# Spectral block on one core: the first run of the last inverse stage stands behind second-stage work of the second sequence, and the second weight is converted sooner

## The chip, the cores and the metric

The kernel runs on one core of one Trainium2 chip. Its five engines take their own instruction lists in order: PE (TensorE, matmuls), DVE (VectorE), ACT (ScalarE), POOL (GpSimd) and SP (SyncE), which in this kernel issues all DMA transfers. They wait for one another by semaphores. The metric is the time of one execution on the device in microseconds; before the change the median of three runs is 1844.56 us (1843.51 to 1845.94).

## The reference

The input x is 8 sequences of 3136 rows by 256 columns, in f32. What is computed, cut to its core:

```python
X = np.fft.rfft(x, axis=1)                       # spectral part
Yr = Xr @ w_r - Xi @ w_i + b_r
Yi = Xr @ w_i + Xi @ w_r + b_i
Yr, Yi = soft_threshold(Yr, 0.01), soft_threshold(Yi, 0.01)
a = np.fft.irfft(Yr + 1j * Yi, n=3136, axis=1)   # f32
mixed = np.real(np.fft.fft(np.fft.fft(a, axis=1), axis=2))
u = a + mixed                                    # mixer
un = (u - mean(u)) / sqrt(var(u) + 1e-6)         # over the 256 columns
out = u + np.maximum(un @ w_ch1, 0) @ w_ch2      # 256 -> 1024 -> 256
```

## The kernel before

A transform of 3136 points is done as two shorter ones, so each sequence b = 0 to 7 goes through three stages. Stage 1 (`p1`) transforms the rows with matmuls against `fwd_f`; ACT copies the result to an xf tile, and SP stores it to DRAM (ad<-xf). Stage 2 goes in four quarters q of eight frequencies each: `rows_f2` loads af and the table tff, `p2_f2` finishes the forward transform (L527, f2 below), `p2_w` multiplies by the complex weights (g_w) and DVE and POOL make the soft threshold (y, m, Y), `p2_yt` transposes Y (g_yt), `p2_g2` makes the first half of the inverse (g_g with table tif; ACT copies it to bev and SP stores it, bd<-bev), and `p2_mix` the mixer (g_mix, mq, stored md<-mq). Stage 3 starts with `p3_norm`: its loads (mt<-md, bf<-bd), the last inverse stage (g_g<-bf,inv_f, L410 in the helper `quarters`), the sum with mt on DVE (ut) and the statistics of the norm. `p3_tr` transposes ut (g_ut) into uth and utl, and two MLP stages multiply by the weights (h, then o). Sequence 0 goes through stage 2 in plain f32 matmuls; from sequence 1 on, an f32 operand is split into a high and a low part (tih and til of tif, say) and three products are summed.

The MLP's weights w1 and w2 come in as eight pieces of 512 KB (raw_w) and are converted on the chip by `split_double` (L200 to L221): one ACT instruction (L200), DVE L201, L203, L205, L207 and L209, and for w2 an ACT cast to the high part w2h (L219) and two DVE instructions to the low part w2l (L220, L221). For w2 `split_double` takes an argument `late`, an instruction of ACT behind which L200 may be issued. Tiles share rooms in SBUF by tag: w2h takes the room with the tag W2 and w2l W3, both held by tiles of stage 1 until these are stored.

What sets the order: each stage is a generator that yields due times, and a heap takes the one with the lowest due time next; `WTIMES` are the due times of the eight weight pieces. A generator can also yield until a key is in the set `done` (`after`). `issue_after` puts an instruction behind another one in the order, and `behind(key, ...)` does so for a DMA issue. A scheduler then fixes each engine's list.

The lines that the change touches most:

```python
quarters(inv_f, groups, w_in[1, 0] if b == 0 and ms[0] == 0 else None)    # L840, p3_norm
behind(3 if b or q else 1, out=tif, in_=c_ti[...])                        # L716, p2_yt
split_double(name, h, l, [(sl, raws.pop(k))], False, ks_in[0, 2 + (k > 5)])   # L942, weights
```

Of the kernel before, what the change touches and what calls it, by code (L numbers as in the profile page):

```python
# [20 lines left out]
D = 256  # L21
# [117 lines left out]
SHAPE, STEP1, STEP = (0.395, 0.569, 0.36), 0.2, 0.25  # L139
START1, LEAD, LAST = 1.61, 1.53, 0.05  # L140
T1, ASK, BEHIND = (1.25, 0.17), 1.16, 3
WTIMES = (1.002, 1.003, 1.151, 1.152, 1.4, 1.44, 1.54, 1.57)
MLAG, NRM, TR = 1.874, -1.239, -0.86


# [1 line left out]
def spectral_block(ctx: ExitStack, tc: tile.TileContext, x, w_ri, b_ri, w1, w2,  # L147
                   c_fwd, c_fwd0, c_inv, c_tf, c_ti, c_cs, c_mask, c_ident, out):
    nc = tc.nc
# [167 lines left out]
    def n2_rows(t, m, n):  # L317

        return t[m:m + n].rearrange("n r c u d -> (r c u) n d")
# [183 lines left out]
    def p2_f2(b):  # L503


        for q in range(4):
            base, STEP, F2W, W0, WW, M0 = clock2(b, q)
            u0 = 8 * q
            yield base
            yield from after(("a", b, q) if b == 0 else ("a", b))  # L510
            if b == 0:
                X = sb.tile([128, 2, 2, 8, S], F32, tag=("Xh", "Xl")[q % 2], bufs=1, name="X")
                Xs = sb.tile([128, 2, 8, S], F32, tag=("Xsh", "Xsl")[q % 2], bufs=1, name="Xs")
                xt[b, q] = X, Xs
            else:
                xt[b, q] = Xh, Xl, Xsh, Xsl = x_tiles()
            afs, tfs = zip(*[rows_f2(b, q, s) for s in range(2)])
            for ui in range(4):
                yield base + STEP * ui * F2W / 4
                us = slice(ui * 2, ui * 2 + 2)  # L520
                lo_x = lo_v if b == 1 and q == 0 else lo_g
                g = gtile("g_f2")
                gf = g[:, :400].rearrange("p (k c s j) -> p k c s j", k=2, c=2, s=2)
                for s in range(2):
                    yield base + STEP * F2W * (ui / 4 + s / 8)
                    for k in range(2):
                        mm = te.matmul(gf[:, k, :, s], afs[s][:, ui * D + k * 128:ui * D + k * 128 + 128],  # L527
                                  tfs[s][:, ui].rearrange("p (c j) -> p c j", c=2), start=True, stop=True)
                    if b == 0 and q == 0 and ui == 0:
                        f2_in[s] = mm.ins  # L530
                        done.add(("f2", s))
                gv = g[:, :400].rearrange("p (k c t) -> p k c t", k=2, c=2)

                def view(t):
                    return t[..., us, :].rearrange("p k c s j -> p k c (s j)" if len(t.shape) == 5 else "p k s j -> p k (s j)")

                if b == 0:
                    xv_ = view(X)
                    sc.copy(xv_, gv)
                    va.tensor_add(view(Xs), xv_[:, :, 0], xv_[:, :, 1])  # L540
                    continue
                xs = sb.tile([128, 2, 2 * S], F32, tag="xs", bufs=2, name="xs")
                xh, xl, xsh, xsl = (view(t) for t in (Xh, Xl, Xsh, Xsl))
                if ui < 3:
                    xx = sb.tile([128, 2, 2, 2 * S], F32, tag="xx", bufs=2, name="xx")
                    sc.copy(xx, gv)
                    sc.copy(xh, xx)  # L547
                    lo_x(xl, xx, xh)
                    va.tensor_add(xs, xx[:, :, 0], xx[:, :, 1])
                else:  # L550
                    im = sb.tile([128, 2, 2 * S], F32, tag="im", bufs=1, name="im")
                    sc.copy(xh, gv)
                    sc.copy(im, gv[:, :, 1])
                    va.tensor_add(xs, gv[:, :, 0], im)
                    lo_v(xl, gv, xh)
                sc.copy(xsh, xs)
                lo_x(xsl, xs, xsh)
# [146 lines left out]
    def p2_yt(b):  # L704

        for q in range(4):
# [4 lines left out]
            for i in range(4):  # L711
                yield base + STEP * (M0 + 0.022 + 0.185 * i)
                s = i // 2
                if i % 2 == 0:
                    tif = sb.tile([100, 4, 98], F32, tag="tif", bufs=2, name="tif")
                    behind(3 if b or q else 1, out=tif, in_=c_ti[:, u0 + 4 * s:u0 + 4 * s + 4, :])  # L716
                    if b == 0:
                        tabs[b, q, s] = tif, None
                    else:
                        tih = sb.tile([100, 4, 98], F32R, tag="tih", bufs=1, name="tih")  # L720
                        til = sb.tile([100, 4, 98], F32R, tag="til", bufs=1, name="til")
                        with tc.issue_after(ks_in[b, q]):
                            sc.copy(tih, tif)
                        lo_v(til, tif, tih)
                        tabs[b, q, s] = tih, til
# [48 lines left out]
    def p3_norm(b):  # L774
# [31 lines left out]
        def load(m, n):  # L806
            mt = sb.tile([128, 4, D], F32, tag="mt", bufs=2, name="mt")
            bfs = [sb.tile([128, 512], F32, tag="bf", bufs=4, name="bf") for _ in range(1 + (n > 1))]
            for r in range(2):
                if n == 1:  # L810
                    nc.sync.dma_start(out=bfs[0][64 * r:64 * r + 64, :D], in_=b_dram[b - 1 + r][m, 0].rearrange("c u d -> (c u) d"))
                else:
                    nc.sync.dma_start(out=bfs[r].rearrange("p (n d) -> p n d", d=D), in_=n2_rows(b_dram[b], m + 2 * r, 2))
            for r in (1, 0):
                bb, n2 = (b - 1 + r, m) if n == 1 else (b, NM * r + m)
                mpn, mmn = (d[0:NH].rearrange("(a n2) d -> a n2 d", n2=N2) for d in m_dram[bb])
# [6 lines left out]
        for ms in pairs + [[NM - 1]] * (b % 2):  # L823
            n = 1 if ms[0] == NM - 1 else 4
            t0, T3 = clock3(b, ms[0])
            yield t0 + T3 * (NRM - 0.5 * (n == 1))
            yield from after(("b", b), ("m", b))
            loads = [load(m, n) for m in ms]
            if n == 1:
                mt, bfs = loads[0]  # L830
                g = gtile("g_g1")
                te.matmul(g[:, :D], inv_f, bfs[0][:, :D], start=True, stop=True)
                add(ms[0], 1, g, mt[:, :1])
                finish(ms[0], 1)
                continue
            if b == 0 and ms[0] == 0:
                yield from after(("w", 1, 0))
            groups = [([gtile("g_g1") for _ in range(2)], [[bfs[r][64 * p:64 * p + 64] for r in range(2)] for p in range(2)], bfs[0][0:1, 0:2])
                      for mt, bfs in loads]
            quarters(inv_f, groups, w_in[1, 0] if b == 0 and ms[0] == 0 else None)  # L840
            parts = [(m + 2 * p, g, mt[:, 2 * p:2 * p + 2]) for m, (mt, bfs), (banks, movs, late) in zip(ms, loads, groups) for p, g in enumerate(banks)]
            for m, g, mt in parts:
                add(m, 2, g, mt)
            for m, g, mt in parts:
                finish(m, 2)

    def p3_tr(b):
        for gi, (g0, z) in enumerate(GROUPS[b % 2]):
            t0, T3 = clock3(b, g0)
            w = z * 128  # L850
            for k in range(2):
                yield t0 + T3 * (TR + k / 4)
                if k == 0:
                    uth = sb.tile([128, 2, 512], F32R, tag="uth", bufs=UTHB, name="uth")
                    utl = sb.tile([128, 2, 512], F32R, tag="utl", bufs=2, name="utl")
# [61 lines left out]
    def weights():  # L917
# [14 lines left out]
        for k, (i, name, sl, src) in enumerate(todo):  # L932
# [6 lines left out]
                l = sb.tile(shape, F32R, tag=f"W{2 * i + 1}", bufs=1, name=name + "l")  # L939
                mlp_w[name] = h, l  # L940
            if i:
                split_double(name, h, l, [(sl, raws.pop(k))], False, ks_in[0, 2 + (k > 5)])  # L942
            elif k % 2:
                mark = (0, k // 2)
                yield from after(("w",) + mark)
# [69 lines left out]
```

## Time and profile before

| what | value |
|---|---|
| median of three runs | 1844.56 us (1843.51 to 1845.94) |
| profiled execution, its own time | 1843.13 us |
| span of the profiled execution | 1841.2 us |
| busy: PE, DVE, ACT, POOL | 1798.6, 1200.5, 807.7, 561.8 us |
| chain of work that ended last | PE 86%, DVE 5%, DMA 4% |
| mean granted clock of PE | 0.993 |

The busy times are shares of the span: PE is busy for 98% of it. The chain is followed back from the last instruction, so its shares say which engine's work set the end. The granted clock is 1.00 at full speed.

### The profile page before, as it was taken

The page shows a single profiled execution, that of the slowest core. Times are in us where ns is not written, and L with a number is a line of the kernel's source. Part 1 is how long each engine was busy: PE and PEld are TensorE (multiplying, and loading weights), DVE is VectorE, ACT ScalarE, POOL GpSimd, SP SyncE. Part 2 cuts the span into 40 slices and gives each one's busy share as a digit, 9 for nine tenths or more (in the row PEclk, how much of TensorE's full clock was granted, in tenths as well). Part 3 has the DMA queues.
Part 4 walks back from the last instruction along what each step waited for, and adds up shares of the span by engine and source line. Part 5 has one row for each costly group of instructions (what it writes and reads, how often), then busy time and mean ns, then how long its engine had stood idle before and what let it go on. Part 6 is the DMA issues. An engine that isn't in the chain of part 4 may idle for free.

```text
span 1841.2 us, 29453 instructions
## 1 busy us (share of the span) xinstructions
PE 1798.6 (98%) x10087; PEld 1498.7 (81%) x10087; DVE 1200.5 (65%) x2619; ACT 807.7 (44%) x1911; POOL 561.8 (31%) x1021
## 2 busy tenths in 40 slices
PE   8987999999999999999999999999999999999998
PEld 5566778888888988888888888888888898878888
DVE  3685686676577766765776667757657767655543
ACT  2664545444445534444444444444444454432222
POOL 0002434333234333343432343423324344222110
PEclk9998999999999999999999999999999999999999
DMA  8856564444436543374515744346533533152211
GB/s 247 272 173 165 165 178 135 148 137 138 130 82 198 159 123 104 97 212 125 172 47 135 215 132 125 104 129 164 159 99 86 169 94 112 56 150 69 59 35 33
DMA packets 157934, 245.61 MB, mean 133 GB/s; under 512 B 24208, under 2 KB 105176, under 8 KB 157528
## 3 DMA queue, kind: packets, MB, share of 16 engines
q1 hardware_dynamic: 157784, 243.72, 45.3%
q8 instruction: 80, 1.31, 0.3%
q14 instruction: 70, 0.57, 0.1%
HBM read 140.79 MB, written 102.86 MB: 132 GB/s over the span
## 4 chain that ended last, share of the span: by engine, by line
PE 86%; DVE 5%; DMA 4%; ACT 1%; SPq 1%; issue 1%; POOL 1%; DVEq 0%; ACTq 0%; POOLq 0%
PE o L175 28%; PE h L175 27%; PE g_w L175 9%; PE g_f L527 5%; PE g_g L175 4%; PE g_yt L730 3%; PE g_g L410 2%; PE g_ut L861 2%; PE g_f L410 2%; PE g_mix L667 1%; DMA out_dram<-total 1%; PE g_f L372 1%; DMA aq<-ev 1%; PE g_mix L669 1%; PE g_w L576 1%
## 5 line engine op out<-in xcount | busy, mean ns | idle before, releaser
L880 DVE SCALAR_TENSOR_TENSOR hl<-h,hh 128x512 fp32r<-128x512 f32 (+2 forms) x416 | 272.1, 655 | 391.2 <-ACT hh L879 386.8
L879 ACT ACTIVATE hh<-h 128x512 fp32r<-128x512 f32 (+2 forms) x416 | 237.7, 572 | 505.7 <-PE h L175 459.4
L175 PE MATMUL o<-hl,w2h 128*128 128x512 f32 (+2 forms) x832 | 328.9, 395 | 2.0 <-DVE hl L880 1.5
L175 PE MATMUL h<-utl,w1h 128*128 128x512 f32 (+2 forms) x832 | 319.0, 383 | 1.3 <-DVE utl L165 1.3
L175 PE MATMUL o<-hh,w2l 128*128 128x512 f32 (+2 forms) x832 | 317.9, 382 | 0.0
L175 PE MATMUL o<-hh,w2h 128*128 128x512 f32 (+2 forms) x832 | 317.3, 381 | 0.0
L175 PE MATMUL h<-uth,w1l 128*128 128x512 f32 (+2 forms) x832 | 316.0, 380 | 0.0
L175 PE MATMUL h<-uth,w1h 128*128 128x512 f32 (+2 forms) x832 | 315.3, 379 | 0.0
L887 POOL TENSOR_TENSOR total<-uth,utl 128x256 f32<-128x256 f32 x200 | 149.6, 772 | 460.6 <-DMA out_dram<-total 244.9
L175 PEld LDWEIGHTS o<-hl,w2h 128*128 128x128 f32 x832 | 156.7, 188 | 49.3 <-DVE hl L880 18.7
L175 PEld LDWEIGHTS h<-utl,w1h 128*128 128x128 f32 x832 | 156.8, 188 | 30.5 <-DVE utl L165 1.7
L175 PEld LDWEIGHTS h<-uth,w1l 128*128 128x128 f32 x832 | 156.7, 188 | 29.5 <-issue 1.6
L175 PEld LDWEIGHTS h<-uth,w1h 128*128 128x128 f32 x832 | 156.9, 189 | 27.7 <-issue 2.4
L175 PEld LDWEIGHTS o<-hh,w2l 128*128 128x128 f32 x832 | 156.5, 188 | 27.2
L175 PEld LDWEIGHTS o<-hh,w2h 128*128 128x128 f32 x832 | 156.9, 189 | 19.8 <-issue 0.8
L527 PE MATMUL g_f<-tff,af 98*128 98x100 f32 x1024 | 139.9, 276 | 2.1 <-DMA af<-aq 1.3
L527 PEld LDWEIGHTS g_f<-tff,af 98*128 98x128 f32 x1024 | 134.2, 195 | 7.8 <-issue 1.7
L593 POOL TENSOR_TENSOR Y<-y,m 128x400 f32<-128x400 f32 x56 | 66.9, 1194 | 208.4 <-DVE m L592 198.6
L590 DVE SCALAR_TENSOR_TENSOR y<-g_w,small,ks 128x400 f32<-128x400 f32 x128 | 80.4, 629 | 54.3 <-PE g_w L175 38.0
L168 POOL TENSOR_TENSOR Xl<-xx,Xh 128x400 fp32r<-128x400 f32 x81 | 88.4, 1092 | 60.3 <-ACT Xh L547 56.8
L761 ACT COPY bev<-g_g 98x512 f32<-98x512 f32 x128 | 74.7, 585 | 40.2 <-PE g_g L175 29.3
L730 PE MATMUL g_yt<-ident,Y 128*100 128x128 f32 x512 | 81.8, 277 | 4.8 <-DVE Y L593 4.6
(162 smaller groups left out, 3269.7 us busy)
## 6 DMA issues: line engine op xcount, KB each, us to landing
bd<-bev SPq DMA_DIRECT2D x128, 196.0 KB
mt<-md SPq DMA_DIRECT2D x192, 128.0 KB
bf<-bd SPq DMA_DIRECT2D x96, 256.0 KB
out_dram<-total SPq DMA_DIRECT2D x88, 256.0 KB
af<-ad SPq DMA_DIRECT2D x56, 392.0 KB
ad<-xf SPq DMA_DIRECT2D x84, 256.0 KB
md<-mq SPq DMA_DIRECT2D x112, 192.0 KB
xf<-in_x SPq DMA_DIRECT2D x39, 512.0 KB
```

The lines of the kernel that those rows point to most:

```text
L168: gp.tensor_sub(out_, full, hi.bitcast(F32))
L175: last = te.matmul(o, l, r, start=start and i == 0, stop=stop and i == 2)
L410: return te.matmul(banks[i][64 * j:64 * j + 64], mat[rows, rows], movs[i][j], start=True, stop=True)
L527: mm = te.matmul(gf[:, k, :, s], afs[s][:, ui * D + k * 128:ui * D + k * 128 + 128], tfs[s][:, ui].rearrange("p (c j) -> p c j", c=2), sta ...
L590: va.scalar_tensor_tensor(y1, gw, bias[:, c, o:o + 1], ks, op0=ALU.add, op1=ALU.add)
L593: (va if b == 0 or o == 0 else gp).tensor_sub(y[:, o, :, c, :], y1, m)
L730: te.transpose(gt[:100, (v * 2 + o) * 128:(v * 2 + o + 1) * 128], y[:, o, place].rearrange("p c j -> p (c j)"), ident)
L761: sc.copy(bev, g[:98])
L861: te.transpose(gv[:, i], ut[:, j, k * 128:(k + 1) * 128], ident)
L879: sc.activation(hh[:, :w], h[:, :w], AF.Relu)
L880: va.scalar_tensor_tensor(hl[:, :w], h[:, :w], 0.0, hh[:, :w].bitcast(F32), op0=ALU.max, op1=ALU.subtract)
L887: gp.tensor_add(total[:, k, cols], uth[:, k, cols].bitcast(F32), utl[:, k, cols].bitcast(F32))
```

## The change

Five edits. The due times of the last four weight pieces, all of w2, are lowered, and the ACT instruction behind which their L200 may be issued becomes that of quarter 1 (and 2) instead of 2 (and 3) of sequence 0. The first inverse run of sequence 0 (four matmuls of L410) may be issued only behind the last f2 matmul of quarter 1 of sequence 1 (`f2_in["last"]`, key "f2"), where before it was behind the first g_w of quarter 0. The tif loads of sequence 1's quarter 0 go behind the first mt load, and wait for a key "norm" that `p3_norm` sets when its first loads are issued. `p3_tr` of sequence 0 waits for a key ("n", 0). The key "bf" of the load in `p3_norm` is set and used nowhere.

```diff
--- before.py
+++ after.py
@@ -139,7 +139,7 @@
 SHAPE, STEP1, STEP = (0.395, 0.569, 0.36), 0.2, 0.25
 START1, LEAD, LAST = 1.61, 1.53, 0.05
 T1, ASK, BEHIND = (1.25, 0.17), 1.16, 3
-WTIMES = (1.002, 1.003, 1.151, 1.152, 1.4, 1.44, 1.54, 1.57)
+WTIMES = (1.002, 1.003, 1.151, 1.152, 1.36, 1.42, 1.48, 1.54)
 MLAG, NRM, TR = 1.874, -1.239, -0.86
 
 
@@ -529,6 +529,9 @@
                     if b == 0 and q == 0 and ui == 0:
                         f2_in[s] = mm.ins
                         done.add(("f2", s))
+                    if b == 1 and q == 1 and ui == 3 and s == 1:
+                        f2_in["last"] = mm.ins
+                        done.add("f2")
                 gv = g[:, :400].rearrange("p (k c t) -> p k c t", k=2, c=2)
 
                 def view(t):
@@ -712,8 +715,10 @@
                 yield base + STEP * (M0 + 0.022 + 0.185 * i)
                 s = i // 2
                 if i % 2 == 0:
+                    if b == 1 and q == 0:
+                        yield from after("norm")
                     tif = sb.tile([100, 4, 98], F32, tag="tif", bufs=2, name="tif")
-                    behind(3 if b or q else 1, out=tif, in_=c_ti[:, u0 + 4 * s:u0 + 4 * s + 4, :])
+                    behind("mt" if b == 1 and q == 0 else 3 if b or q else 1, out=tif, in_=c_ti[:, u0 + 4 * s:u0 + 4 * s + 4, :])
                     if b == 0:
                         tabs[b, q, s] = tif, None
                     else:
@@ -810,7 +815,7 @@
                 if n == 1:
                     nc.sync.dma_start(out=bfs[0][64 * r:64 * r + 64, :D], in_=b_dram[b - 1 + r][m, 0].rearrange("c u d -> (c u) d"))
                 else:
-                    nc.sync.dma_start(out=bfs[r].rearrange("p (n d) -> p n d", d=D), in_=n2_rows(b_dram[b], m + 2 * r, 2))
+                    af_ld["bf"] = nc.sync.dma_start(out=bfs[r].rearrange("p (n d) -> p n d", d=D), in_=n2_rows(b_dram[b], m + 2 * r, 2)).ins
             for r in (1, 0):
                 bb, n2 = (b - 1 + r, m) if n == 1 else (b, NM * r + m)
                 mpn, mmn = (d[0:NH].rearrange("(a n2) d -> a n2 d", n2=N2) for d in m_dram[bb])
@@ -826,6 +831,7 @@
             yield t0 + T3 * (NRM - 0.5 * (n == 1))
             yield from after(("b", b), ("m", b))
             loads = [load(m, n) for m in ms]
+            done.add("norm")
             if n == 1:
                 mt, bfs = loads[0]
                 g = gtile("g_g1")
@@ -834,15 +840,16 @@
                 finish(ms[0], 1)
                 continue
             if b == 0 and ms[0] == 0:
-                yield from after(("w", 1, 0))
+                yield from after("f2")
             groups = [([gtile("g_g1") for _ in range(2)], [[bfs[r][64 * p:64 * p + 64] for r in range(2)] for p in range(2)], bfs[0][0:1, 0:2])
                       for mt, bfs in loads]
-            quarters(inv_f, groups, w_in[1, 0] if b == 0 and ms[0] == 0 else None)
+            quarters(inv_f, groups, f2_in["last"] if b == 0 and ms[0] == 0 else None)
             parts = [(m + 2 * p, g, mt[:, 2 * p:2 * p + 2]) for m, (mt, bfs), (banks, movs, late) in zip(ms, loads, groups) for p, g in enumerate(banks)]
             for m, g, mt in parts:
                 add(m, 2, g, mt)
             for m, g, mt in parts:
                 finish(m, 2)
+            done.add(("n", b))
 
     def p3_tr(b):
         for gi, (g0, z) in enumerate(GROUPS[b % 2]):
@@ -850,6 +857,8 @@
             w = z * 128
             for k in range(2):
                 yield t0 + T3 * (TR + k / 4)
+                if b == gi == 0:
+                    yield from after(("n", 0))
                 if k == 0:
                     uth = sb.tile([128, 2, 512], F32R, tag="uth", bufs=UTHB, name="uth")
                     utl = sb.tile([128, 2, 512], F32R, tag="utl", bufs=2, name="utl")
@@ -939,7 +948,7 @@
                 l = sb.tile(shape, F32R, tag=f"W{2 * i + 1}", bufs=1, name=name + "l")
                 mlp_w[name] = h, l
             if i:
-                split_double(name, h, l, [(sl, raws.pop(k))], False, ks_in[0, 2 + (k > 5)])
+                split_double(name, h, l, [(sl, raws.pop(k))], False, ks_in[0, 1 + (k > 5)])
             elif k % 2:
                 mark = (0, k // 2)
                 yield from after(("w",) + mark)
```

ACT at 63 us, where bev is the copy of sequence 0's inverse half, mq the mixer's copy, xf the copies of stage 1, and raw_w_772 the fifth weight piece (k = 4). Before:

```order
L411 COPY g_f_590<-xf 1x2
L761 COPY bev<-g_g_570 98x512
L671 COPY mq<-g_mix 100x256
L469 COPY xf<-g_f_589 128x512
L469 COPY xf<-g_f_590 128x512
L219 CAST w1h<-cv_w_ut 128x512
L411 COPY g_f_646<-xf 1x2
L219 CAST w1h<-cv_w_ut 128x512
```

and now:

```order
L411 COPY g_f_590<-xf 1x2
L766 COPY bev<-g_g_570 98x512
L200 ACTIVATE cv_w_mt<-raw_w_772 128x512
L674 COPY mq<-g_mix 100x256
L200 ACTIVATE cv_w_mt<-raw_w_869 128x512
L469 COPY xf<-g_f_589 128x512
L469 COPY xf<-g_f_590 128x512
L411 COPY g_f_646<-xf 1x2
L219 CAST w1h<-cv_w_ut 128x512
```

Two L200 of w2 have come in, one ahead of the mq copy and one ahead of the xf copies; before, they stood some 26 us further down, at 89 us.

SP at 135 us, the loads around stage 3's start (md_117 and bd_118 are the DRAM tiles of sequence 0). Before:

```order
L763 DMA bd_118<-bev 98x512 x2
L309 DMA tif<-c_ti 100x392
L818 DMA mt<-md_117 32x4x256
L819 DMA mt<-md_117 32x1024
L818 DMA mt<-md_117 32x4x256
L763 DMA bd_118<-bev 98x512 x2
L819 DMA mt<-md_117 32x1024
L495 DMA af<-ad_116 98x1024 x2
L813 DMA bf<-bd_118 128x2x256 x2
```

and now:

```order
L768 DMA bd_118<-bev 98x512 x2
L495 DMA af<-ad_116 98x1024
L823 DMA mt<-md_117 32x4x256
L824 DMA mt<-md_117 32x1024
L823 DMA mt<-md_117 32x4x256
L768 DMA bd_118<-bev 98x512 x2
L824 DMA mt<-md_117 32x1024
L309 DMA tif<-c_ti 100x392
L495 DMA af<-ad_116 98x1024
L497 DMA tff<-c_tf 98x400
L818 DMA bf<-bd_118 128x2x256 x2
```

The tif load has moved from ahead of the first mt loads to behind the fourth of them, and one af load ahead of them.

PE at 145 us, behind the g_w block of sequence 1's quarter 0. Before:

```order
L175 MATMUL g_w<-Xl,wdh 128x400
L175 MATMUL g_w<-Xh,wdl 128x400
L410 MATMUL g_g_1377<-bf,inv_f 64x512
L410 MATMUL g_g_1378<-bf,inv_f 64x512
L410 MATMUL g_g_1377<-bf,inv_f 64x512
L410 MATMUL g_g_1378<-bf,inv_f 64x512
L730 MATMUL g_yt<-ident,Y 100x128
L527 MATMUL g_f_1461<-tff,af 128x2x50 x4
L527 MATMUL g_f_1474<-tff,af 128x2x50 x4
L730 MATMUL g_yt<-ident,Y 100x128
L527 MATMUL g_f_1496<-tff,af 128x2x50 x4
```

and now:

```order
L175 MATMUL g_w<-Xl,wdh 128x400
L175 MATMUL g_w<-Xh,wdl 128x400
L735 MATMUL g_yt<-ident,Y 100x128
L527 MATMUL g_f_1419<-tff,af 128x2x50 x4
L527 MATMUL g_f_1432<-tff,af 128x2x50 x4
L735 MATMUL g_yt<-ident,Y 100x128
L527 MATMUL g_f_1454<-tff,af 128x2x50 x4
L735 MATMUL g_yt<-ident,Y 100x128 x6
```

and 11 rows further down:

```order
L735 MATMUL g_yt<-ident,Y 100x128 x4
L670 MATMUL g_mix<-cs,eh 100x256
L672 MATMUL g_mix<-cs,el 100x128
L410 MATMUL g_g_1513<-bf,inv_f 64x512
L410 MATMUL g_g_1514<-bf,inv_f 64x512
L410 MATMUL g_g_1513<-bf,inv_f 64x512
L410 MATMUL g_g_1514<-bf,inv_f 64x512
L870 MATMUL g_ut<-ident,ut 128x128 x4
```

The four inverse matmuls of the list (the trace counts each as two) stood right behind g_w; now a g_yt, three f2 groups, six g_yt, a g_g and two g_mix stand ahead of them.

## Rows read from the trace of the kernel before

**Rows 1.** Table by stretch: length, busy us (instructions) PE PEld DVE ACT POOL, PEclk, DMA, GB/s.
```profile
60.00:100.00 40.00, 37.70 (x208) 23.25 (x207) 29.01 (x66) 24.64 (x61) 0.00 (x0) 1.00 0.78 244
...
114.00:130.00 16.00, 10.56 (x50) 8.03 (x49) 14.93 (x40) 8.65 (x23) 0.00 (x0) 0.79 0.32 91
...
145.00:176.00 31.00, 21.55 (x110) 17.82 (x109) 18.74 (x44) 14.65 (x34) 13.74 (x25) 0.72 0.71 177
...
300.00:1841.20 1541.20, 1530.32 (x8663) 1296.59 (x8661) 1002.48 (x2172) 662.23 (x1567) 501.79 (x912) 1.00 0.42 122
```

**Rows 2.** SP timeline, 58 to 78 us: start, us, engine, line, transfer.
```profile
60.67 1.16 SPq L309 DMA_DIRECT2D raw_w<-in_w  x2
```

**Rows 3.** Chain of waits, 25 to 100 us: start, us, what.
```profile
33.53 6.74 DMA raw_w<-in_w
...
84.18 5.24 DMA tff<-c_tf
...
92.94 2.96 DMA ad<-xf
```

**Rows 4.** ACT timeline, 62 to 82 us; in brackets: idle before, and releaser.
```profile
63.24 0.59 ACT L761 COPY bev<-g_g 98x512 f32<-98x512 f32 x1 [0.99 <-PE g_g L757]
63.73 0.38 ACT L671 COPY mq<-g_mix 100x256 f32<-100x256 f32 x1
67.19 1.07 ACT L469 COPY xf<-g_f 128x512 f32<-128x512 f32 x2 [3.09 <-DMA raw_w<-in_w]
```

**Rows 5.** PE timeline, 63 to 100 us.
```profile
67.36 1.51 PE L576 MATMUL g_w<-X,wdf 128*128 128x400 f32 x4
...
70.11 1.09 PE L410 MATMUL g_f<-xf,fwd_f 64*64 64x512 f32 x8
...
75.00 2.82 PE L527 MATMUL g_f<-tff,af 98*128 98x100 f32 x24
...
86.14 1.51 PE L576 MATMUL g_w<-X,wdf 128*128 128x400 f32 x4
```

**Rows 6.** DVE groups, 40 to 130 us: busy us, mean ns, idle before.
```profile
L205 DVE SCALAR_TENSOR_TENSOR cv_w_ut<-raw_w,cv_w_mt 128x512 int32<-128x512 int32 x8 | 5.5, 686 | 0.0
...
L207 DVE TENSOR_SCALAR cv_w_mt<-cv_w_ut 128x512 int32<-128x512 int32 x8 | 3.4, 420 | 0.0
```

**Rows 7.** PE timeline, 117 to 132 us.
```profile
121.70 0.87 PE L664 MATMUL g_mix<-csf,ef 128*100 128x129 f32 x6 [2.51 <-DVE mq L676]
124.64 0.88 PE L730 MATMUL g_yt<-ident,Y 128*100 128x128 f32 x3 [2.06 <-DVE Y L593]
126.38 2.54 PE L664 MATMUL g_mix<-csf,ef 128*100 128x129 f32 x10 [0.86 <-ACT yf L734]
...
129.57 2.12 PE L527 MATMUL g_f<-tff,af 98*128 98x100 f32 x16
```

**Rows 8.** Table by two us (and four), columns of group 1.
```profile
124.00:126.00 2.00, 0.88 (x3) 0.45 (x3) 2.00 (x6) 1.87 (x4) 0.00 (x0) 0.50 0.00 0
```

**Rows 9.** PE timeline, 143 to 176 us.
```profile
153.09 2.10 PE L410 MATMUL g_g<-bf,inv_f 64*64 64x512 f32 x8 [7.39 <-DMA bf<-bd]
155.12 0.45 PE L730 MATMUL g_yt<-ident,Y 128*100 128x128 f32 x1
...
174.28 0.34 PE L175 MATMUL g_w<-Xsh,wrh 128*128 128x400 f32 x1
```

**Rows 10.** Chain of waits, 125 to 176 us.
```profile
142.70 3.40 DMA bd<-bev
...
146.60 6.36 DMA bf<-bd
```

**Rows 11.** SP timeline, 134 to 148 us.
```profile
136.68 2.26 SPq L309 DMA_DIRECT2D tif<-c_ti  x1
...
143.14 0.40 SPq L819 DMA_DIRECT2D mt<-md  x1
```

**Rows 12.** DVE timeline, 142 to 158 us.
```profile
144.53 0.56 DVE L165 TENSOR_TENSOR til<-tif,tih 100x392 fp32r<-100x392 f32 x1
```

## Prediction

> **What bounds the kernel now.** I read the page's busy shares first, then the table by stretch, and after it the timelines of each stretch in which PE stands. The reader is to see two things in the table [rows 1]. From 300 us to the end PE is busy for 1530.32 of 1541.20 us, at full clock: there it is the bound, with 10.9 us of idle in all. The change's instructions lie ahead of 200 us, and behind that both programs issue the same work in the same order on every engine. So what the change wins or loses ahead of 200 us reaches the end nearly whole, and the sum is the shift of PE at the point where the two orders are the same again. The second thing: the stretches that the change touches are those where PE is not the bound. It idles 2.3 us of 60–100 us, 5.4 us of 114–130, and 9.5 us of 145–176, with the granted clock at 0.79 and 0.72 in the last two [rows 1]. Each engine takes its list in order, so I walk along three of them.
>
> **Part A, 63 to 98 us: two conversions come sooner, +11 us.** The first two pieces of the second weight are converted behind the bev copy that ACT starts at 63.24 us [rows 4], about 26 us sooner. On ACT the conversion's first instruction (L200) now stands between that bev copy and the mq copy of 63.73, which waited for nothing but PE. L200 needs raw_w, and SP issued both of those loads at 60.67 [rows 2]. A load of the same size (512 KB) took 6.74 us from issue to landing [rows 3]; by that the first one lands at 60.67 + 6.74 = 67.4 us, and ACT's idle of 3.09 us in before, put down to raw_w and ended at 67.19, says the same [rows 4]. So ACT stands from 63.83 to 67.4 with everything behind L200 queued: the mq copy, the xf copies, the casts of the first weight.
>
> - Step 1. L200 ends near 68.1 (an estimate of 0.7 us for it, from bev's 0.59 on the same number of columns [rows 4]), the mq copy near 68.5, then DVE's small mq instruction, and PE's g_w<-X,wdf (67.36 [rows 5]) starts near 69.5: +2.
> - Step 2. The second L200 stands ahead of the xf copies and waits for DVE to read the buffer of the first; DVE can only begin when L200 ended, and has two instructions of 0.42, a y and one of 0.69 ahead [rows 6]. That puts the xf copies of 67.19 at about 71.5 (+4.4), and with the weight casts and DVE pieces between them the f2 block that starts PE's 70.11 row at about 75.5: +5.4 [rows 5].
> - Step 3. The cast into w2h takes room W2, which the tile of first-stage rows holds until its four stores have landed. The last of them is issued near 77.7 in the shifted schedule, and a store of that kind took 2.96 us [rows 3], so the cast starts at 80.6, ahead of copies that PE's f2 (75.00 [rows 5]) needs: f2 at about 81.7, +6.7.
> - Step 4. The subtraction into w2l does the same on DVE with room W3: stores issued near 91, landed 2.96 to 5.24 us later [rows 3], 94 to 96.2. The y for PE's g_w of 86.14 stands behind it. Two w2l pieces and that y (0.69 + 0.69 + 0.63 less overlap) put g_w at 97 to 98: +11 to +12.
>
> I take +11 for part A. Its bounds: if none of the waits binds, the pieces cost nothing on PE, as DVE has 11 us free in 60–100 us [rows 1]; if the second landing is like the tff load's 5.24, +12.5. The later conversions (k=6, 7) stand where k=4, 5 stood, so the small PE stalls after 90 us stay.
>
> The Trainium skill ("DMA: Bandwidth & Descriptors", section "Anatomy of one DMA") puts a transfer at about 2 us plus its bytes at 436 GB/s; it gives that fit for the GpSimd path. By it 512 KB would land 3.2 us after the issue, at 63.9, and step 1 would cost nothing; the trace's 6.74 us for the same load, with the DMA engines at a share of 0.78 in this stretch [rows 1, 3], speaks against it. It is a rival below, since a landing at 64 can be had from no row.
>
> **Part B, 114 to 130 us: the same two conversions are gone, -3.7 us.** One conversion is three instructions of 0.42 and four of 0.69 us on DVE, 4.0 us [rows 6], and two of them ran from 114.9 to 128 us, where DVE was busy for 14.93 of 16 us [rows 1]. PE waits there three times: 2.51 us for mq, 2.06 for Y (both DVE's), 0.86 for ACT's yf, 5.43 us together, and the clock falls to 0.50 [rows 7, 8]. Without the 8 us, DVE's chain from y to Y is done about 3 us sooner, yet PE's g_mix still has to wait for the mq copies that follow it on ACT. Walking the list, f2 (129.57 [rows 7]) comes at 125.2 to 126.5: a gain of 3 to 4.4, and I take 3.7. The lower bound is 0 (ACT ends last in each of the waits), the upper 5.4 (all idle gone).
>
> **Part C, 145 to 176 us: the first inverse run behind f2, -1.6 us.** PE stands 7.39 us after its g_w block, from 145.7 to 153.09, for the bf load; then come the eight inverse matmuls, and only then a g_yt (155.12) and the f2 of the second sequence [rows 9]. The chain is a bd store of 3.40 us and a bf load of 6.36 [rows 10], whatever PE does. The change lets g_yt, f2, g_g and g_mix of sequence 1 stand ahead of the inverse, so the 7.39 us could be filled, if their inputs are there. They are later than before: the tif load of (1, 0) was issued at 136.68 and now stands behind the last of the first mt loads (143.14 + 0.40) [rows 11]. Landing 3.40 (as bd) to 6.36 us (as bf) later [rows 10], it is there at 147 to 150; I take 147.5, since tif is smaller than either (153 KB). Its cast and DVE's til (0.56, at 144.53 [rows 12]) stand ahead of Y on DVE; til can start at about 148.3, so Y is about 4 us late, and the first g_yt is at about 151 instead of 155.12, the inverse at about 161.4 instead of 153.09. With 4 us of useful work moved ahead and the slow clock (0.72 in the mean [rows 1]) lifted no sooner than before, the two orders are level at about 172.7 instead of 174.28 [rows 9]: -1.6. Bounds: -4 (Y is not delayed by tif, PE's gap shrinks to 3 us) and +4 (the inverse is 8 us late, its output feeds the transposes and the MLP, and these find nothing to fill PE with).
>
> **The sum.** 11 - 3.7 - 1.6 = +5.7 us. The profiled execution took 1843.13 us (span 1841.2 us); with the change 1848.8. The median of the runs, 1844.56, lies 1.4 us above it, so for a median 1850.2; I say 1850. Differences under 0.2% (3.7 us) can't be told from no change here.
>
> **Rivals.**
>
> - *The room waits don't bind (no change).* Step 1 and 2 happen (+5), steps 3 and 4 are covered, since in before the tiles of W2 and W3 had to be written in the same stretch too. For it: DVE and ACT are idle for 11 and 15 us of 60–100 [rows 1]. Against: both instructions are in order ahead of copies that PE needs. 5 - 3.7 - 1.6 = -0.3, 1844.
> - *The conversions fall into idle time (faster).* One mechanism: raw_w lands before ACT comes to L200 at 63.83. Then L200 runs in the 3.09 us in which ACT stands in before [rows 4], the stores keep their times, and the room waits end before their instructions are reached; part A costs about 1 us. For it: a landing in 3.40 us, like the bd store's [rows 10], would be 64.1. Against: the 6.74 and the 3.09. It decides from a landing of about 64.5 on: 1 - 3.7 - 1.6 = -4.3, 1840; with part B at its upper end 1838. The Trainium skill's fit above (3.2 us) would give this case.
> - *The inverse run comes too late (much slower).* Part C at +4 with A as forecast: 11 - 3.7 + 4 = +11, 1856. For it: 8 us of delay for the first MLP inputs. Against: f2 and g_yt of sequence 1 are work that PE has to do anyway.
> - *The wait is only replaced.* In place of the bf load PE waits for Y behind til, 7.39 again, and C is 0: 11 - 3.7 = +7.3, 1852, inside the forecast's own range.
>
> **Chances.** Forecast (with the replaced wait) 0.50, own range 1846.5 to 1854; no change 0.20; faster 0.23; much slower 0.07. Faster by over 0.2%: the faster case, with a little of the no-change case, 0.24. Within 0.2%: no change and the low end of the forecast, 0.22. Slower: 0.54. The range that holds 8 in 10 leaves out the ends of the faster and the much slower case: 1839 to 1855.
>
> **What would show it.** Step 1: on ACT an idle of 3 to 4 us ahead of the first L200 of w2, with releaser raw_w. Steps 3 and 4: the first w2h cast and w2l subtraction with an idle released by the ad stores, and g_w<-X,wdf that was at 86.14 at 97. Part B: DVE busy less than 10 of the 16 us around f2, PE idles there under 2 us. Part C: the gap after the g_w block 5 to 6 us and ended by DVE's Y, not by bf; the first inverse matmul 8 us later in relation to the g_w block. The forecast is wrong if the rows of 70 to 98 us are within 3 us of before: then A failed; or if PE runs on from g_w into g_yt with no gap: then C was too small.

## The result, and the profile after

The changed kernel takes 1859.45 us (median of 4 runs, 1856.96 to 1860.21), the kernel before 1845.25 us beside it: a ratio of 1.0073 (95% interval 1.0056 to 1.0091), some 14 us slower. Run again beside other kernels it took 1860.48 us, 1.0084 (1.0067 to 1.0101). The direction was forecast, the size was not: +5.7 us, with 1846.5 to 1854 as the forecast's own range and 1855 as the upper end of the wider one.

The table by stretch of the changed kernel, as in [rows 1] (columns: length, busy us of PE, PEld, DVE, ACT, POOL, then PEclk, DMA share, GB/s):

```profile
60.00:100.00 40.00, 32.78 (x159) 19.28 (x157) 24.31 (x57) 20.28 (x49) 0.00 (x0) 0.87 0.72 216
...
300.00:1858.40 1558.40, 1547.97 (x8766) 1310.91 (x8764) 1017.15 (x2209) 672.04 (x1593) 509.54 (x928) 1.00 0.42 122
```

In the last row the two kernels are alike: 10.4 us of PE idle from 300 us on, 10.9 before [rows 1]. All of the loss is ahead of it, and most of it in 60 to 100 us, where PE was busy for 37.70 us at full clock and is now for 32.78 at 0.87. Step 1 of the forecast is there, larger than forecast. The load of raw_w on SP, and ACT behind it (compare [rows 2, 4]):

```profile
65.45 1.69 SPq L309 DMA_DIRECT2D raw_w<-in_w  x2
```

```profile
65.42 0.58 ACT L766 COPY bev<-g_g 98x512 f32<-98x512 f32 x1 [0.99 <-PE g_g L762]
72.77 0.66 ACT L200 ACTIVATE cv_w_mt<-raw_w 128x512 f32<-128x512 f32 x1 [6.76 <-DMA raw_w<-in_w]
73.33 0.36 ACT L674 COPY mq<-g_mix 100x256 f32<-100x256 f32 x1
75.53 0.68 ACT L200 ACTIVATE cv_w_mt<-raw_w 128x512 f32<-128x512 f32 x1 [1.84 <-DVE cv_w_ut L205]
...
85.90 0.62 ACT L219 CAST w2h<-cv_w_ut 128x512 fp32r<-128x512 f32 x1 [1.46 <-DMA ad<-xf]
```

ACT ends bev at 66.0 and stands 6.76 us for raw_w; the second L200 waits for DVE's L205 as forecast, and w2h's cast for the ad stores (step 3). On DVE the subtraction into w2l stood too (step 4; this trace names tif as the last to come, the second profile of the kernel the ad stores, with an idle of 4.06 us):

```profile
101.57 1.29 DVE L221 TENSOR_TENSOR w2l<-cv_w_ut 128x512 fp32r<-128x512 f32 x2 [3.84 <-DMA tif<-c_ti]
```

What PE does with that (compare [rows 5, 7, 9]):

```profile
74.01 3.04 PE L579 MATMUL g_w<-X,wdf 128*128 128x400 f32 x4 [4.30 <-DVE mq L679]
76.84 1.91 PE L762 MATMUL g_g<-yf,tif 100*98 100x256 f32 x4
...
87.06 2.92 PE L527 MATMUL g_f<-tff,af 98*128 98x100 f32 x24 [1.32 <-ACT xf L469]
...
103.47 2.62 PE L579 MATMUL g_w<-X,wdf 128*128 128x400 f32 x4 [3.99 <-DVE mq L679]
...
147.04 2.53 PE L527 MATMUL g_f<-tff,af 98*128 98x100 f32 x16
...
167.78 0.45 PE L735 MATMUL g_yt<-ident,Y 128*100 128x128 f32 x1 [4.39 <-POOL Y L603]
...
181.95 1.99 PE L410 MATMUL g_g<-bf,inv_f 64*64 64x512 f32 x8 [0.78 <-ACT low L676]
```

Two gaps of 4.30 and 3.99 us, both ended by DVE's mq, stand where forecast, ahead of the two g_w<-X,wdf. What was not forecast stands right behind them: four matmuls of g_w take 3.04 us in place of 1.51 [rows 5], the next four g_g 1.91 in place of 1.03. That is the half clock, 1.2 GHz: the granted clock of 74 to 88 us is 0.66 in the mean.

A table of landmarks on PE shows where the time goes: starts in us, from the PE timelines. The first column is the kernel before, "again" the second run of the changed one.

| PE row | before | changed | again | conversions alone | inverse alone |
|---|---|---|---|---|---|
| g_w<-X,wdf, the one before the first wait | 58.6 | 60.8 | 57.8 | 58.4 | 60.1 |
| next g_w<-X,wdf (67.36 in [rows 5]) | 67.4 | 74.0 | 71.7 | 68.3 | 68.9 |
| f2 x24 (75.00) | 75.0 | 87.1 | 84.6 | 81.5 | 76.5 |
| g_w<-X,wdf (86.14) | 86.1 | 103.5 | 101.2 | 97.8 | 87.6 |
| f2 x24 | 98.7 | 117.8 | 115.4 | 113.0 | 100.2 |
| last g_w<-X,wdf of sequence 0 | 116.3 | 137.1 | 134.7 | 130.6 | 117.8 |
| f2 x16 (129.57 in [rows 7]) | 129.6 | 147.0 | 144.9 | 140.8 | 131.1 |
| first g_w of sequence 1 | 138.9 | 156.6 | 154.2 | 152.9 | 140.4 |
| 48th o | 211.2 | 229.2 | 228.9 | 221.6 | 214.7 |
| span | 1841.2 | 1858.4 | 1858.2 | 1852.6 | 1844.1 |

The first line is startup: it lies between 57.8 and 60.8 us in these profiles, and shifts below are counted from it (an "again" of 71.7, say, is 71.7 + 0.8 against 67.4).

### The profile page after: what moved, and what is told of

Same layout as the page of the kernel before. It is cut to its first block, busy times and chain, and to the rows that moved or that the text cites. A ratio compares the mean times of both kernels' runs of the same rounds, so it can differ in the third digit from the quotient of the medians.

```text
span 1858.4 us, 29450 instructions
## 1 busy us (share of the span) xinstructions
PE 1811.3 (97%) x10087; PEld 1507.9 (81%) x10087; DVE 1198.8 (65%) x2619; ACT 807.4 (43%) x1911; POOL 560.4 (30%) x1021
## 4 chain that ended last, share of the span: by engine, by line
PE 88%; DVE 5%; DMA 3%; ACT 2%; SPq 1%; issue 1%; POOL 1%; DVEq 0%; ACTq 0%; POOLq 0%
PE o L175 28%; PE h L175 27%; PE g_w L175 9%; PE g_f L527 5%; PE g_g L175 4%; PE g_yt L735 3%; PE g_g L410 2%; PE g_ut L870 2%; PE g_f L410 2%; PE g_w L579 2%; PE g_mix L670 1%; PE g_mix L672 1%; DMA out_dram<-total 1%; DVE ut L784 1%; DMA mt<-md 0%
## 5 line engine op out<-in xcount | busy, mean ns | idle before, releaser
L175 PEld LDWEIGHTS h<-uth,w1h 128*128 128x128 f32 x832 | 156.6, 188 | 27.8 <-issue 2.4
L527 PEld LDWEIGHTS g_f<-tff,af 98*128 98x128 f32 x1024 | 138.3, 201 | 9.0 <-issue 2.1
```

The lines of the kernel that those rows point to most:

```text
L175: last = te.matmul(o, l, r, start=start and i == 0, stop=stop and i == 2)
```

## The experiments

**The two halves of the change.** They can be built apart; PE's order up to 190 us is then that of before or after, but for three g_yt near 72 us that go with the conversions. Conversions alone:

```diff
+WTIMES = (1.002, 1.003, 1.151, 1.152, 1.36, 1.42, 1.48, 1.54)
+split_double(name, h, l, [(sl, raws.pop(k))], False, ks_in[0, 1 + (k > 5)])
 quarters(inv_f, groups, w_in[1, 0] if b == 0 and ms[0] == 0 else None)   # as before
```

> Only the weight conversions are moved (due times and the ACT instruction behind which L200 may go); the first inverse run stays where it was in the kernel before. Theory 1 (nearly all of the loss is the conversions): +13 to +16 us against before, 1858 to 1861, with the PE gaps of about 4 us ahead of both g_w<-X,wdf (at 74 and 103 us) and the half clock behind them as in the changed kernel. Rival (the later inverse run loses its part, +4): +9 to +11 us, 1854 to 1856.

Measured: 1854.15 us, 1.0057 (1.0034 to 1.0079), +10.5 us by the ratio and +8.8 by the medians. That lies at the rival's figure. It does not show that the inverse stage's edit has a part in the loss, as the interval overlaps the changed kernel's. On SP and PE:

```profile
46.79 1.19 SPq L309 DMA_DIRECT2D xf<-in_x  x2
...
59.34 0.92 SPq L309 DMA_DIRECT2D raw_w<-in_w  x2
```

```profile
68.27 1.61 PE L576 MATMUL g_w<-X,wdf 128*128 128x400 f32 x4 [1.01 <-DVE mq L676]
...
76.14 2.03 PE L527 MATMUL g_f<-tff,af 98*128 98x100 f32 x8 [0.56 <-DVE mq L676]
78.10 1.99 PE L410 MATMUL g_f<-xf,fwd_f 64*64 64x512 f32 x8
...
81.54 3.28 PE L527 MATMUL g_f<-tff,af 98*128 98x100 f32 x24
...
97.78 3.04 PE L576 MATMUL g_w<-X,wdf 128*128 128x400 f32 x4 [4.13 <-DVE mq L676]
...
163.79 1.66 PE L410 MATMUL g_g<-bf,inv_f 64*64 64x512 f32 x8 [4.09 <-DMA bf<-bd]
```

Here raw_w was issued at 59.34 and landed at 66.95, and the shifts are those of the forecast: f2 x24 +6.8 (forecast +6.7), g_w at 97.78 +11.9 (forecast 11 to 12). At f2 this is in part luck. The stage-1 group of 70.11 [rows 5] is 4.4 us late where step 2 has 5.4 (and calls it f2), and f2 x24 waits for nothing, where step 3 has it wait for a room. What made up the difference is the half clock, for which the forecast has no term: the stage-1 group of 78.10 takes 1.99 us in place of 1.09, the f2 x8 ahead of it 2.03 in place of 1.03. Then the half clock (3.04) makes it +14.6 at the next f2 x24. At 163.79 the wait for bf is 4.09 us in place of 7.39 [rows 9]: the transfers set that start, so 3.3 us of the lateness are absorbed there.

The inverse stage's edit alone (the weights as in before):

> Only the first inverse run, the tif loads and the first transposes are moved; the weights are converted where they were before. Theory 1: -2 to +1 us against before, since PE still waits 4 to 5 us behind the g_w block, now for Y. Prediction on record: -1.6 us (-4 to +4). Rival (the inverse comes too late and the MLP starts late): +4 us. 60 to 145 us should be as in the kernel before, startup included, if the slower startup seen in the changed kernel's trace has nothing to do with this edit.

Measured: 1844.51 us beside 1845.33, 1.0004 (0.9991 to 1.0018): no change by itself, and no gain. The mechanism is part C's, and up to the first g_yt its times too: til on DVE is late and the first g_yt waits until 151.4 (counted from startup; forecast 151), for a Y that the trace puts on POOL. The inverse comes 12.5 us later, not 8 (14 us in the rows, 1.5 of it startup):

```profile
149.90 0.57 DVE L165 TENSOR_TENSOR til<-tif,tih 100x392 fp32r<-100x392 f32 x1 [3.79 <-ACT tih L728]
```

```profile
152.88 0.45 PE L735 MATMUL g_yt<-ident,Y 128*100 128x128 f32 x1 [5.69 <-POOL Y L603]
...
167.04 1.99 PE L410 MATMUL g_g<-bf,inv_f 64*64 64x512 f32 x8 [0.78 <-ACT low L676]
```

Behind it the clock, too, differs from the forecast. The table by stretch of this run, and then the same rows of the kernel before:

```profile
164.00:168.00 4.00, 3.22 (x20) 2.35 (x18) 1.93 (x5) 2.72 (x6) 0.61 (x1) 0.50 0.71 204
168.00:172.00 4.00, 3.21 (x18) 2.19 (x11) 2.90 (x10) 0.69 (x2) 0.19 (x1) 0.50 0.81 254
172.00:176.00 4.00, 4.00 (x19) 3.69 (x19) 3.23 (x11) 3.02 (x7) 3.10 (x11) 0.56 0.75 223
```

```profile
164.00:168.00 4.00, 3.78 (x13) 3.16 (x14) 2.82 (x6) 2.20 (x7) 3.71 (x6) 0.56 0.00 0
168.00:172.00 4.00, 3.22 (x28) 2.86 (x27) 2.01 (x5) 2.99 (x8) 1.48 (x6) 1.00 0.54 136
```

In before the full clock is back by 168 us, while the first MLP matmuls run (from 164.2); here PE waits again, 1.60, 0.78 and 0.79 us ahead of 161.5, 167.0 and 169.8, the clock stays at half until about 175, and the MLP's matmuls, which need the inverse, start at 176.2. From the first g_w of sequence 1 to the 48th o this profile loses 2.0 us (214.7 - 140.4 against 211.2 - 138.9). How much of that is the clock and how much the waits, no run here tells apart.

**tif undone.** As the inverse edit alone, without the edit to the tif load:

```diff
-if b == 1 and q == 0:
-    yield from after("norm")
-behind("mt" if b == 1 and q == 0 else 3 if b or q else 1, out=tif, ...)
+behind(3 if b or q else 1, out=tif, ...)
```

> As the run with the inverse stage's edit alone (inv_only, 1844.5 us), but the tif loads of the second sequence's first quarter are issued where the kernel before has them. Theory 4 (the gap of 5.7 us behind the g_w block is Y's, which stands behind til on DVE and so behind tif): that gap falls to under 2.5 us, 3 to 4 us faster than inv_only: 1840.5 to 1842. Rival (Y is late for another reason, or the gap only moves to the bf load further down): the time stays within 1.5 us of inv_only.

Measured: 1848.62 us, 1.0026 (1.0008 to 1.0044); the rival held, and more.

```profile
148.81 0.31 PE L733 MATMUL g_yt<-ident,Y 128*100 128x128 f32 x1 [1.80 <-POOL Y L603]
151.26 1.15 PE L527 MATMUL g_f<-tff,af 98*128 98x100 f32 x4 [2.14 <-DMA af<-ad]
156.28 2.88 PE L527 MATMUL g_f<-tff,af 98*128 98x100 f32 x12 [3.88 <-DMA tff<-c_tf]
```

Y's gap fell from 5.69 to 1.80 us as theory 4 said, but PE then waited 2.14 us for af and 3.88 for tff, which stand behind tif in SP's list. Without the tif edit the time is some 4 us longer, though the two intervals just overlap: PE's waits in this stretch only pass from one load to another.

**raw_w sooner.** Conversions alone, with the loads of pieces 5 and 6 issued some 10 us sooner (49 to 51 us):

```diff
-behind(("q1", "q1", 3, 3, 5, 5, 5, 5)[k], out=raw..., in_=src)
+behind(("q1", "q1", 3, 3, 3, 3, 5, 5)[k], out=raw..., in_=src)
```

> As the run with the conversions alone (w2_only, 1854.2 us), but the loads raw_w of its fifth and sixth piece are issued behind the af load of quarter 1 (some 20 us sooner), so that they have landed before ACT comes to L200. Theory 1 (the wait for raw_w with the queues behind it is the first half of the loss): no ACT idle ahead of L200, PE's two gaps between 66 and 76 us (1.0 and 2.6 us) gone, 4 to 7 us faster: 1847 to 1850. Rival (the waits for rooms W2 and W3 are the bound of 70 to 100 us, wherever the first one ends): the 4 us gap ahead of the third g_w<-X,wdf stays or grows, and the time is within 2 us of w2_only.

Measured: 1847.93 us, 1.0027 (1.0013 to 1.0041), against 1.0057 without it: some 5.5 us back by the ratios, 4.5 by the medians. On ACT and PE:

```profile
64.78 0.69 ACT L200 ACTIVATE cv_w_mt<-raw_w 128x512 f32<-128x512 f32 x1 [0.57 <-DVE cv_w_ut L205]
...
67.62 0.68 ACT L200 ACTIVATE cv_w_mt<-raw_w 128x512 f32<-128x512 f32 x1 [1.41 <-DVE cv_w_ut L205]
```

```profile
69.32 1.50 PE L576 MATMUL g_w<-X,wdf 128*128 128x400 f32 x4
...
80.24 5.44 PE L527 MATMUL g_f<-tff,af 98*128 98x100 f32 x24 [0.62 <-ACT xf L469]
```

L200 no longer waits for raw_w (0.57 us for DVE is left), g_w starts without a gap, and the 4 us gap further down is gone too: the rival fell. Several small gaps are left, and f2 x24 takes 5.44 us in place of 2.82 [rows 5], at half clock. What the other 5 us are made of, no run separates. The same edit in the changed kernel:

> The changed kernel with the two raw_w loads issued sooner (as in raw_early). Theory 1: the same gain as there, 5 to 6 us against the changed kernel, 1853 to 1855, as the wait for raw_w and what follows from it is independent of the inverse stage. Rival (with the inverse run moved, PE waits for Y and the loads behind 145 us whatever came before, so the gain is lost there): within 2 us of the changed kernel.

Measured: 1851.77 us, 1.0040 (1.0025 to 1.0056), against 1.0084 for the changed kernel beside it: 8.7 us back, more than expected. In its profile the first g_w of sequence 1 is 6.2 us late in place of 15.5 and 16.2, so the gain lies ahead of the inverse stage, and the rival fell.

**The rooms.** Conversions alone, with the two early casts into w2h held back:

```diff
+with tc.issue_after(cast) if cast is not None else nullcontext():   # ks_in[0, 2] for k < 6
     sc.copy(h[sl], v(wf, sl))
```

> As the run with the conversions alone, but the casts of the two early conversions into w2h (and with them the subtractions into w2l) may go only behind the ks copy of quarter 2, as before; L200 to L209 stay early. Theory 3 (the waits for rooms W2 and W3 are worth their two PE gaps, 1.3 and 4.0 us, and the clock behind the second): 4 to 7 us faster than with the conversions alone. Rival (the delay of 67 to 75 us, the raw_w load and its queue on ACT and DVE, is all that matters, and it pushes the rest): within 2 us of it.

Measured: 1855.23 us, 1.0056 (1.0037 to 1.0075). The gap of 4.13 us was gone from PE and one of 2.13 us stood elsewhere, so the waits for rooms are real, but the time is that of the conversions alone: theory 3 has no gain to show. The profiles can't settle it, as raw_w was issued at 64.4 us in this one.

**The clock.** In the conversions alone, 20 matmuls behind the last mean (the tile is never read):

```diff
+warm = ps.tile([128, 512], F32, tag="h", bufs=2, name="warm")
+with tc.issue_after(last.ins):
+    for i in range(20):
+        te.matmul(warm, idle[:, :128], idle, start=True, stop=True)
```

> As the run with the conversions alone, with 20 matmuls on a constant tile (output not used) put on PE into the first gap, behind the last mean matmul at 69 us, so that PE is busy while it waits for the mq copy behind L200. Theory 2 (a part of the loss is the clock, which fell to half in 74 to 84 us, where the same groups took 3.04, 1.91, 1.07, 1.98 us in place of 1.51, 1.03, 0.60, 1.09): 3 to 5 us faster than with the conversions alone, clock 1.00 in 74 to 84. Rival (ACT and DVE are late in any case and PE only waits longer for them): within 1 us of the run with the conversions alone.

Measured: 1860.16 us, 1.0085 (1.0064 to 1.0105), slower than without.

```profile
66.72 4.74 PE L220 MATMUL warm<-idle 128*128 128x512 f32 x20
71.29 1.50 PE L581 MATMUL g_w<-X,wdf 128*128 128x400 f32 x4
...
80.08 1.98 PE L415 MATMUL g_f<-xf,fwd_f 64*64 64x512 f32 x8 [5.97 <-DVE y L595]
```

The gap is filled and g_w runs in 1.50 us, but the scheduler put ACT's and DVE's instructions in another order behind it, and a gap of 5.97 us for y follows at half clock. So it tells nothing of the clock's price in 70 to 100 us.

The same in the kernel before, 28 matmuls behind the g_w block of sequence 1's quarter 0, in the 7.39 us of [rows 9]:

```diff
+if b == 1 and q == 0:
+    with tc.issue_after(w_in[1, 0]):
+        for i in range(28):
+            te.matmul(warm, idle[:, :128], idle, start=True, stop=True)
```

> The kernel before, with 28 matmuls on a constant tile (output not used) put on PE behind the g_w block of the second sequence's quarter 0, in the 7.4 us in which PE waits for bf. Theory 2 (what follows ran at half clock from 152 to 167 us because PE stood, and that costs time): clock 1.00 from 150 on, 3 to 6 us faster than before: 1839 to 1842. Rival (DVE and ACT set the pace there, so a faster PE waits more): within 1.5 us of before, with PE gaps grown by what the matmuls save.

Measured: 1838.54 us, 0.9971 (0.9957 to 0.9984): faster than both kernels, by 5 us against before.

```profile
148.71 6.53 PE L599 MATMUL warm<-idle 128*128 128x512 f32 x28
155.93 1.21 PE L410 MATMUL g_g<-bf,inv_f 64*64 64x512 f32 x8 [0.69 <-DMA bf<-bd]
```

```profile
152.00:156.00 4.00, 3.31 (x16) 2.45 (x15) 2.70 (x6) 0.88 (x3) 1.27 (x2) 1.00 1.06 279
156.00:160.00 4.00, 4.00 (x34) 3.09 (x35) 3.01 (x9) 2.60 (x7) 0.23 (x1) 1.00 1.00 240
```

and in before:

```profile
152.00:156.00 4.00, 2.91 (x13) 1.34 (x13) 0.78 (x2) 0.08 (x1) 0.00 (x0) 0.50 0.99 239
156.00:160.00 4.00, 4.00 (x21) 4.00 (x20) 3.40 (x11) 2.01 (x5) 2.31 (x3) 0.50 0.96 232
```

The inverse starts 0.69 us after the last of them, takes 1.21 us in place of 2.10 [rows 9], and the clock is 1.00 where it was 0.50. The scheduler also put the first MLP matmuls behind a g_g and two g_mix, so how many of the 5 us are the clock's is not shown. With ten more behind the last g_w of sequence 0:

> The kernel before with the 28 matmuls of bef_warm (1838.5 us) and 10 more behind the last g_w of sequence 0, ahead of the g_g and g_mix at 117 us, to hold the clock through 120 to 130 us, where DVE keeps PE waiting 5.4 us. Theory 2: the clock stays at 1.00 through 122 to 130 and f2 comes 1 to 2 us sooner: 1836.5 to 1838. Rival (the ten delay g_mix, on which DVE's mq waits, by their own 2 us): 0 to 2 us slower than bef_warm.

Measured: 1840.29 us, 0.9976 (0.9964 to 0.9988): not told apart from bef_warm, and no gain as theory 2 had it. The same filling with the inverse moved:

> The inverse stage's edit alone (inv_only) with 20 such matmuls in the gap behind the same g_w block. Theory 2: the clock, which fell to half from about 152 to 176 us in inv_only, stays up; 4 to 7 us faster than inv_only: 1837.5 to 1840.5, and then the inverse edit is worth its 1.6 us and more once the clock is held. Rival: within 1.5 us of inv_only.

Measured: 1845.13 us, 1.0015 (1.0003 to 1.0027): the rival, no faster than without. The clock was at half all the same from 156 to 168 us. And in the changed kernel with raw_w sooner:

> The same with 20 matmuls on a constant tile (output not used) in PE's gap behind the g_w block of sequence 1's quarter 0. Theory 5 (with the inverse run moved, the MLP's first matmuls come 12 us later in the list, and till then PE has too little work to hold the clock): the clock still falls to half some 10 us later, and the time is within 2 us of after_early. Rival (one gap decides the clock, as in the kernel before, where filling it gave 5 us): 4 to 6 us faster than after_early.

Measured: 1852.91 us, 1.0040 (1.0025 to 1.0055), as without. Its table by stretch:

```profile
164.00:168.00 4.00, 2.29 (x17) 1.71 (x16) 3.23 (x7) 3.32 (x9) 2.17 (x4) 1.00 0.40 104
168.00:172.00 4.00, 2.83 (x13) 2.83 (x14) 2.31 (x4) 3.02 (x8) 3.00 (x5) 0.63 0.00 0
172.00:176.00 4.00, 3.60 (x18) 1.87 (x17) 1.94 (x5) 1.92 (x6) 0.98 (x2) 0.51 0.73 222
```

The clock is held to 168 us and falls then, behind new gaps (PE is busy for 2.29 of 4 us and waits 2.38 for DVE's yl). Theory 5 holds as far as the time goes: with the inverse late, filling the first gap moved the fall of the clock and did not remove it.

**The changed kernel again.**

> The changed kernel once more, beside the other three on one chip, with a second profile of it. If the slow startup of its first profile (clock 0.55 in 28 to 36 us, first g_w 2 us late) is chance, this profile has the first g_w at 30 to 33 us, raw_w's load issued near 60 and ACT's wait ahead of L200 at 3 to 4 us in place of 6.8, and a time of 1855 to 1858; if it belongs to the program, it shows again and the time is 1859 to 1861.

Measured: 1860.48 us. The slow startup did not come again (first g_w at 30.4 us), yet the time is the one expected if it had: the raw_w load was late without it.

```profile
47.18 1.17 SPq L309 DMA_DIRECT2D xf<-in_x  x2
...
63.47 0.92 SPq L309 DMA_DIRECT2D raw_w<-in_w  x2
```

```profile
70.49 0.66 ACT L200 ACTIVATE cv_w_mt<-raw_w 128x512 f32<-128x512 f32 x1 [7.51 <-DMA raw_w<-in_w]
```

```profile
71.73 3.03 PE L579 MATMUL g_w<-X,wdf 128*128 128x400 f32 x4 [5.05 <-DVE mq L679]
```

SP issued raw_w 16.3 us after the second pair of xf loads here, 12.6 in the conversions alone. The trace puts SP's wait ahead of raw_w, 4.5 us, down to an xf load; in the changed kernel's first profile it is 3.7, in before 1.0, and in the conversions alone SP does not wait there. The spread is not the conversions' own: the wait is 3.0 us with matmuls filled into the kernel before, and 3.9 with them and the inverse moved. What sets it stays open.

## Why the prediction was wrong, step by step

**Where PE is not the bound: right.** The loss is all ahead of 200 us and reaches the end: +18.0 at the 48th o and +17.2 in the span of the first profile.

**Part A, +11: the waits right, two terms wrong.** The waits of steps 1, 2 and 4 are in the trace on PE; that of step 3 is there on ACT, and on PE in the changed kernel alone (1.32 us).

First, when raw_w is issued was read off one execution, at 60.67 [rows 2], where nothing depended on it. In the kernels' profiles it lies between 59.3 and 65.5; in the two of the changed kernel at 65.45 and 63.47. Its landing took 7.2 and 6.9 us, near the 6.74 taken [rows 3]. Counted from startup the load landed 3.1 and 3.9 us later than the forecast's 67.4, and the shift at the g_w of 86.14 was +15.2 and +15.9 in place of the +11.9 of the conversions alone, where it landed when forecast. The 3.09 us that ACT idled in before [rows 4] were no second sign of that landing, though the trace named raw_w. With the inverse alone the same idle stands ahead of the same copy, and PE's stage-1 group ends it; in before that group ends at 67.10, just ahead of the copy at 67.19:

```profile
68.69 1.07 ACT L469 COPY xf<-g_f 128x512 f32<-128x512 f32 x2 [3.09 <-PE g_f L410]
```

```profile
66.01 1.09 PE L410 MATMUL g_f<-xf,fwd_f 64*64 64x512 f32 x8
```

Second, no term was there for the clock behind the new gaps: 3.04 and 1.91 us in place of 1.51 and 1.03 behind the first, and +2.7 between the second and the next f2 x24 in the conversions alone. Together part A is +14.6 to the last g_w of sequence 0 there, and +18.6 and +19.3 in the changed kernel. Filling the gap in that stretch put another gap in its place, so what the clock alone costs there is read from the rows and not shown by a run.

**Part B, -3.7: right in its size.** From that last g_w to f2 x16 the gain is 3.3 us (18.6 to 15.3), 3.1 again (19.3 to 16.2) and 3.1 with the conversions alone (14.6 to 11.5). With the conversions alone half clock from f2 x16 on gave most of it back (the first g_w of sequence 1 is 14.3 late); in the changed kernel it held. There, in the 16 us around f2, DVE is busy for 10.1 us in place of 14.93 and PE idles 2.75 in place of 5.44 [rows 1]; the forecast said under 10 and under 2.

**Part C, -1.6: the failed step is the time at which the two orders are level.** til, Y and g_yt came as worked out, but the inverse came 12.5 us later in place of 8, the clock rose 6.5 us later than in before (8 in the rows, 1.5 of it startup) where the sum has it no different, and the stretch cost 2.0 us alone, and 0.3 and 2.4 in the two profiles of the changed kernel: no gain in any. It also took away a cover that the forecast did not see: where the inverse stands behind g_w, the wait for bf absorbs 3.3 us of what part A loses; where g_yt waits for Y behind tif, whose load follows the late mt loads, nothing is absorbed. The landmarks show this, the times do not: the changed kernel (1.0073 and 1.0084) is not clearly slower than the conversions alone (1.0057, 1.0034 to 1.0079), and 3 to 4 us of what divides their profiles is the later landing of raw_w.

**The rivals.** "The room waits don't bind" fell: w2l waited 3.84 us, and the g_w behind it 3.99. "The conversions fall into idle time" had its deciding point right: a landing by 64.5 us. It never came by itself; made by an earlier issue, 5.5 of 10.5 us came back, not all, so the one mechanism did not hold the whole of part A. The Trainium skill's fit ("DMA: Bandwidth & Descriptors", section "Anatomy of one DMA", 3.2 us by it for 512 KB), which the page gives for the GpSimd path, does not describe these loads of SP: they took 6.9 to 7.6 us. "The wait is only replaced" was half of part C: Y's gap is 5.69 and 4.39 us, not 7.39. "The inverse run comes too late" (+4, 1856) was given the least chance and was the nearest of the cases in its time, but by luck: it has part A as forecast and the loss in part C, and most of the loss beyond the forecast is part A's.

The sum as measured, from startup on to the 48th o: 18.6 - 3.3 + 0.2 (to the first g_w) + 0.3 = 15.8 in the first profile and 19.3 - 3.1 + 2.4 = 18.6 in the second, against 11 - 3.7 - 1.6 = 5.7. The medians say 14 to 16.

## What to carry to other kernels

Where an instruction is moved ahead in an in-order list so that it comes to depend on a transfer on which nothing hung before, price the transfer's spread, not one execution's time, and the work queued behind it. Check a releaser that a trace names against another run of the same wait: the one that came last may be a coincidence. Add the clock to every gap that a change makes: read from the trace what the same group takes at either level. And a wait that is bound by transfers, not by the work ahead of it, hides lateness from upstream, 3.3 us here; before removing it, ask what it was absorbing.

## What the runs showed of the hardware that was not expected

A gap of 7.4 us on PE had a price behind it as well: filled with 28 matmuls on a constant tile, 6.53 us in all, the kernel before became 5 us faster, though the inverse behind the gap still waited for its load. The Trainium skill ("TensorE: Matmul & The Clock Gate", section "What's actually happening") says that the slow level is the default and activity lifts it; the rows agree, 0.50 in 152 to 160 us in before, behind the gap, and 1.00 there with the added matmuls. One filled gap was not enough where others followed: in the changed kernel with raw_w sooner PE waited again behind it, 2.38 us for yl among them, and the clock fell to 0.51.
